# Delta rule and two MLP layers on one core: order of the start and of the first block rewritten

## The chip, the cores and the metric

One core of a Trainium2 chip. The metric is the device time of one execution in microseconds (us).

## The reference, cut to what matters

```python
k_n = k / (norm(k) + 1e-6)                       # q, k, v: 4 batches, 8 heads, 768 steps, 48 wide
for t in range(S):
    y[t] = q[t] @ state                          # state: 48x48 per batch and head
    state += beta[t] * outer(k_n[t], v[t] - k_n[t] @ state)
x = y as [3072 tokens, 384]
x = elu(x @ w_in) @ w_out                        # 384 -> 2048 -> 384
out = swish_1.702(x @ w_in2) @ w_out2
```

## The kernel before

**The work.** The 768 steps are cut into 12 chunks of 64 (`NC`), two chunks to a pass (`NP` = 6 passes of 128 steps). A pass begins with two Gram products (`gram`, L169, k against k, 128 small matmuls on PE each, evacuated by ACT at L182), from which `inverse` (L187) makes the norms and inverts 32x32 triangular blocks on DVE: `take` L205 (transpose), `diag` L210, `root` L221 to L223 and three times `better` L227 to L230 (a square root by Newton's steps), `norm` L234 to L242, `scale` L246, 14 row steps L262/L267 (passes 0 to 2, "fine"), `finish` L271/L272, `turn` L278. For the fine passes `join16` puts 16-wide halves together (transpose L292, `left` L299, `right` L307 to L309). Then a chunk's steps (`chunk`, from L315): `kq` (L342, with a masking on DVE at L348), `t2` L355, `m1` L364, `m2` L379, `nv` L332, `ks` L395/L400, `w` L408/L413, `state` L423/L426, `y` L434/L439, `out` (transposes L454, split into a high and a low part at L459/L460). Chunk c needs the state of chunk c-1.

**The layers.** The MLP runs in 192 units: for either layer, for 6 blocks of 512 tokens, for 16 slices of the hidden width. A unit is `up` (9 matmuls 128x512, L531, into a bank of PSUM), the activation (ACT L540, L541, DVE L544, ACT L553, DVE L556) and, two units later (`LAG`), `down` (9 matmuls, L565). Weights arrive as 64-bit words (`raw`, 768 KB a slice) and are made into a high and a low part by `prep`: `rebase` (ACT L489), `shift` and `rest` (DVE L496, L499), `high` (ACT L506), `low` (DVE L510). Unit t of the first block can't start before slice t is converted; later blocks of the layer use the same weights.

**The order.** It is written by hand in `schedule`, and each engine's queue is served in that order. Before unit 0 stands a start: loads, Gram products, `inverse` of pass 0, both chunks of pass 0 (chunk 1 without its `state`) and 20 of the 48 conversion steps. From unit 0 on four lists give what is put in at each unit: `fill` (after the activation's first half, mainly DVE work), `mid` (before `down`), `end` (after it); `spread` shares out a list over units by given sizes. In the block of units 0 to 15 the code puts the other 28 conversion steps (units 0 to 7), `inverse` of pass 1 (units 0 to 6), the chunks 2 and 3 (units 1 to 14, most of it from unit 8), the Gram products of pass 2 (units 8 and 10) and 3 (13 and 15), and `inverse` of pass 2 from unit 11. Block 1 (units 16 to 31) has chunks 4 and 5, still with `join16`, and `inverse` of pass 3 from unit 19. From unit 32 a block has two chunks, two Gram products and no joins.

**Buffers.** The chunk steps share one double bank of PSUM (`wide`, tile ps_w) and one single bank (`bank`, ps_b; in the start also the units' two h banks). The units' three accumulators acc0 to acc2 stand unused until unit 2. SP issues all loads, in order; the first ones are k of chunks 0 and 1, then q, weights, v at once.

Of the kernel before, what the change touches and what calls it, by code (L numbers as in the profile page):

```python
# [20 lines left out]
P = 128  # L21
# [10 lines left out]
class Kernel:  # L32
# [112 lines left out]
    def load_q(self, c):  # L145
# [41 lines left out]
    def inverse(self, p, spare=None):  # L187
# [29 lines left out]
        def root():  # L217

            a, q = small("na"), small("nb")
            s["a"], s["q"] = a, q  # L220
            v.tensor_scalar(out=a, in0=s["d"], scalar1=1e-30, scalar2=None, op0=ALU.max)  # L221
            v.tensor_scalar(out=q.bitcast(U32), in0=a.bitcast(U32), scalar1=1, scalar2=None, op0=ALU.logical_shift_right)
            v.tensor_scalar(out=q, in0=q, scalar1=2.0**64 / 1.457, scalar2=None, op0=ALU.mult)  # L223

        def better():
            a, q = s["a"], s["q"]
            v.reciprocal(out=a, in_=q)  # L227
            v.tensor_tensor(out=a, in0=a, in1=s["d"], op=ALU.mult)
            v.tensor_tensor(out=a, in0=a, in1=q, op=ALU.add)
            v.tensor_scalar(out=q, in0=a, scalar1=0.5, scalar2=None, op0=ALU.mult)  # L230
# [50 lines left out]
        return [start, take, diag, root, better, better, better, norm, scale] + rows + [finish, turn]  # L281
# [33 lines left out]
    def chunk(self, c):  # L315
# [20 lines left out]
        def kq(ps=None):  # L336
            ps = self.wide() if ps is None else ps
            for u in range(8):
                for hf, ab in self.turns():
                    k = self.w_half(hf, ab)  # L340
                    r = 64 * (1 - k)
                    pe.matmul(  # L342
                        ps[self.tok(k), hf, 64 * u:64 * u + 64], g["kt"][r:r + D, 8 * hf + u, :],
                        g["x"][k][r:r + D, 8 * hf + u, :], start=True, stop=True,
                    )
            for k in range(2):
                r = self.tok(k)
                v.tensor_tensor(  # L348
                    out=g["x"][k][r], in0=ps[r].rearrange("p f (u t) -> p (f u) t", u=8),
                    in1=self.mask_p[r].unsqueeze(1).to_broadcast([64, 16, 64]), op=ALU.mult,  # L350
                )
# [50 lines left out]
        def w():  # L402
            ps = self.wide()
            z = s["z"][:, us, :]
            for u in range(8):
                for hf, ab in self.order():
                    k, t = self.w_half(hf, ab), self.tok(ab)
                    pe.matmul(  # L408
                        ps[self.tok(k), hf, hs(u)], z[t, 8 * hf + u, :], st["r"][t, hf, hs(u)],
                        start=True, stop=True,  # L410
                    )
            for k in range(2):
                act.copy(su[k][self.tok(k)], ps[self.tok(k), :, 0:HB])  # L413
# [14 lines left out]
        def y():  # L428
            st["y"] = ap.tile([P, 2, HB], F32, name="y", tag="ry", bufs=2)
            ps = self.wide()  # L430
            for u in range(8):
                for hf, ab in self.order():
                    k = self.w_half(hf, ab)
                    pe.matmul(  # L434
                        ps[self.tok(ab), hf, hs(u)], g["x"][k][:, 8 * hf + u, :], su[k][:, hf, hs(u)],
# [3 lines left out]
            act.copy(  # L439
                st["y"].rearrange("p i (f x) -> p f i x", f=2),  # L440
                ps[:, :, 0:HB].rearrange("p f (i x) -> p f i x", i=2),
            )
# [19 lines left out]
        return dict(nv=nv, t2=t2, m1=m1, kq=kq, m2=m2, ks=ks, w=w, state=state, y=y, out=out)  # L462
# [179 lines left out]
    def schedule(self):  # L642

# [3 lines left out]
        mid, end, fill = {}, {}, {}  # L647
# [19 lines left out]
        names = ("nv", "t2", "m1", "kq", "m2", "ks", "w", "state", "y", "out")  # L667
# [34 lines left out]
        loads[1]()  # L702
        self.load_v(0)
        self.load_v(1, "ry", 2)
        self.load_kn(0)
        loads[2]()
        self.constants()
        self.gram(0, self.grp[0]["kt"])
        self.gram(1, self.grp[1]["kt"])
        for f in steps[0:3]:  # L710
            f()
        ch[0]["kq"]()
        for f in steps[3:8]:
            f()
# [15 lines left out]
        convert(2)  # L730
# [47 lines left out]
        for slot, c, name in (  # L778
# [3 lines left out]
        ):  # L782
# [7 lines left out]
        for p in range(2, NP):  # L790
            o = base[p - 1]
            a, b = 2 * p, 2 * p + 1
            for slot, c, name in (
# [5 lines left out]
                at(end if slot % 2 else mid, u, ch[c][name])  # L799
# [32 lines left out]
        for t in range(len(units) + self.LAG):  # L832
# [44 lines left out]
    def sizes(self, p):  # L877

        rows = [0.14 + j * (15 - j) / 240 for j in range(1, 15)] if p in self.FINE else [0.14 + j * (31 - j) / 480 for j in range(1, 31)]
        return [0.1, 1.9, 0.2, 0.7, 1.0, 1.0, 1.0, 1.7, 1.2] + rows + [1.4, 1.9]  # L880
# [102 lines left out]
```

## Time and profile before

| | us |
|---|---|
| median of 3 runs (lowest, highest) | 1098.32 (1095.07, 1101.81) |
| the profiled execution | 1102.94 |
| its span | 1101.2 |
| busy: PE, DVE, ACT, POOL | 1015.4, 594.8, 452.4, 49.2 |
| granted TensorE clock, mean | 0.966 |

Of the profiled execution 1.7 us lie outside the span. The busy shares are averages over a start without large matmuls, a first block in which three kinds of work meet, and a long part in which PE is busy nearly without a break.

### The profile page before, as it was taken

The numbers are of one execution on the slowest core, as the hardware profiler recorded it, in microseconds if no ns is written. First come the engines' busy times: TensorE is split into PE (matmuls) and PEld (weight loads), VectorE is DVE, ScalarE is ACT, GpSimd is POOL, SyncE is SP. The second block draws the span as 40 slices with busy tenths as digits, with TensorE's granted clock in tenths as the row PEclk, the third lists the DMA queues.
The fourth block names the chain that finished last, engine by engine and source line by source line (L and its number), as shares of the span: only waits on it lengthen the run. The fifth ranks groups of instructions, "written<-read, shape, count | busy, mean of one in ns | idle before, by whom it ended". The sixth has DMA issues, their size and how long they took to land.

```text
span 1101.2 us, 26885 instructions
## 1 busy us (share of the span) xinstructions
PE 1015.4 (92%) x12136; PEld 866.1 (79%) x12136; DVE 594.8 (54%) x1047; ACT 452.4 (41%) x733; POOL 49.2 (4%) x65
## 2 busy tenths in 40 slices
PE   4377688897999999999999899999999999999997
PEld 4365567776888788888888788899999999999996
DVE  3648971665577677777643366673333333333332
ACT  2245343343445534444544466553333333233332
POOL 2000000000000100000000000010000001000000
PEclk9997876998999999999999999999999999999999
DMA  8435001140113022121110190101002020020101
GB/s 271 178 153 162 1 2 36 36 126 32 60 52 94 18 82 60 51 77 49 42 31 1 73 407 37 58 1 35 24 1 58 1 58 1 1 58 1 29 1 29
DMA packets 20563, 68.41 MB, mean 62 GB/s; under 512 B 3552, under 2 KB 6624, under 8 KB 20448
## 3 DMA queue, kind: packets, MB, share of 16 engines
q1 hardware_dynamic: 20448, 66.69, 18.2%
q8 instruction: 95, 1.56, 0.6%
q14 instruction: 20, 0.16, 0.0%
HBM read 57.25 MB, written 9.44 MB: 61 GB/s over the span
## 4 chain that ended last, share of the span: by engine, by line
PE 86%; DVE 8%; issue 3%; ACT 2%; DMA 1%; ACTq 0%; DVEq 0%
PE h L531 35%; PE acc L565 17%; PE acc L576 9%; PE accn L576 9%; PE ps_w L434 3%; PE ps_w L342 2%; PE ps_w L180 2%; PE ps_w L423 1%; PE ps_b L364 1%; PE ps_b L379 1%; PE ps_w L395 1%; PE ps_w L408 1%; DVE tmp L262 1%; DVE W L267 1%; DVE x L348 1%
## 5 line engine op out<-in xcount | busy, mean ns | idle before, releaser
L531 PE MATMUL h<-xh,wt 128*128 128x512 f32 x1152 | 401.6, 403 | 0.6 <-ACT xh L459 0.6
L531 PEld LDWEIGHTS h<-xh,wt 128*128 128x128 f32 x1152 | 220.0, 191 | 47.0 <-ACT xh L459 1.0
L531 PE MATMUL h<-xl,wt 128*128 128x512 f32 x576 | 229.4, 398 | 0.0
L565 PE MATMUL acc<-gh,wt 128*128 128x512 f32 x576 | 203.7, 408 | 3.1 <-ACT xo L629 2.6
L553 ACT CAST gh<-t 128x512 fp32r<-128x512 f32 x192 | 119.2, 621 | 174.0 <-DVE t L544 117.9
L556 DVE TENSOR_TENSOR gl<-t,gh 128x512 fp32r<-128x512 f32 x192 | 138.4, 721 | 67.9 <-PE acc L576 29.5
L550 DVE TENSOR_TENSOR t<-t,h 128x512 f32<-128x512 f32 x96 | 66.0, 688 | 180.3 <-ACT t L547 180.1
L547 ACT ACTIVATE t<-h 128x512 f32<-128x512 f32 x96 | 57.4, 598 | 198.9 <-PE h L531 198.9
L565 PEld LDWEIGHTS acc<-gh,wt 128*128 128x128 f32 x576 | 112.6, 196 | 28.3 <-ACT xo L629 3.0
L565 PE MATMUL acc<-gl,wt 128*128 128x512 f32 x288 | 117.3, 407 | 15.1 <-DVE gl L556 15.1
L531 PEld LDWEIGHTS h<-xl,wt 128*128 128x128 f32 x576 | 110.0, 191 | 19.6 <-DVE xl L460 0.3
L540 ACT ACTIVATE t<-h 128x512 f32<-128x512 f32 x96 | 57.3, 597 | 136.4 <-PE h L531 136.0
L544 DVE SCALAR_TENSOR_TENSOR t<-t,h 128x512 f32<-128x512 f32 x96 | 65.4, 681 | 72.4 <-ACT t L541 72.0
L576 PE MATMUL acc<-wt,gh 128*128 128x384 f32 x384 | 98.4, 337 | 0.0
L576 PE MATMUL accn<-wt,gh 128*128 128x384 f32 x384 | 98.0, 336 | 0.0
L565 PEld LDWEIGHTS acc<-gl,wt 128*128 128x128 f32 x288 | 56.5, 196 | 28.5 <-DVE gl L556 17.6
L576 PEld LDWEIGHTS accn<-wt,gh 128*128 128x128 f32 x384 | 70.9, 188 | 5.5
L576 PEld LDWEIGHTS acc<-wt,gh 128*128 128x128 f32 x384 | 70.3, 188 | 2.8
L576 PE MATMUL acc<-wt,gl 128*128 128x384 f32 x192 | 64.8, 338 | 0.0
L576 PE MATMUL accn<-wt,gl 128*128 128x384 f32 x192 | 64.7, 337 | 0.0
L541 ACT ACTIVATE t<-t 128x512 f32<-128x512 f32 x96 | 60.7, 632 | 3.1
L593 POOL TENSOR_TENSOR xl<-x1r,xh 128x512 fp32r<-128x512 f32 x18 | 24.1, 1338 | 415.8 <-ACT xh L592 322.1
(126 smaller groups left out, 983.2 us busy)
## 6 DMA issues: line engine op xcount, KB each, us to landing
raw<-in_w SPq DMA_DIRECT2D x32, 768.0 KB, 9.9
kt<-in_kT SPq DMA_DIRECT2D x12, 512.0 KB, 4.7
x<-in_qT SPq DMA_DIRECT2D x24, 256.0 KB, 5.0
kg<-in_kT SPq DMA_DIRECT2D x10, 512.0 KB, 4.1
vn<-in_vn SPq DMA_DIRECT2D x12, 384.0 KB, 3.4
kn<-in_kn SPq DMA_DIRECT2D x12, 384.0 KB, 3.2
x1d<-xo SPq DMA_DIRECT2D x12, 384.0 KB, 2.8
x1r<-x1d SPq DMA_DIRECT2D x6, 768.0 KB, 4.6
```

The lines of the kernel that those rows point to most:

```text
L434: pe.matmul(ps[self.tok(ab), hf, hs(u)], g["x"][k][:, 8 * hf + u, :], su[k][:, hf, hs(u)], start=True, stop=True,)
L531: nc.tensor.matmul(hps, wt[:, part, k * P:(k + 1) * P], src[:, k, c], start=(i == 0), stop=(i == 3 * NK - 1))
L540: nc.scalar.activation(out=t, in_=hps, func=AF.Relu, scale=-1.0)
L541: nc.scalar.activation(out=t, in_=t, func=AF.Exp, scale=-1.0)
L544: nc.vector.scalar_tensor_tensor(out=t, in0=t, scalar=-1.0, in1=hps, op0=ALU.add, op1=ALU.max)
L547: nc.scalar.activation(out=t, in_=hps, func=AF.Sigmoid, scale=1.702)
L550: nc.vector.tensor_tensor(out=t, in0=t, in1=hps, op=ALU.mult)
L553: nc.scalar.copy(gh, t)
L556: nc.vector.tensor_tensor(out=gl, in0=t, in1=gh.bitcast(F32), op=ALU.subtract)
L565: self.nc.tensor.matmul(acc[c], wt[:, part, DM + c * P:DM + (c + 1) * P], src, start=(m == 0 and i == 0), stop=(m == NM - 1 and i == 2),)
L576: self.nc.tensor.matmul(acc[w], src[:, c], wt[:, part, DM:2 * DM], start=(m == 0 and i == 0), stop=(m == NM - 1 and i == 2),)
L593: nc.gpsimd.tensor_tensor(out=xl[:, c, :], in0=st["raw"][:, c, :], in1=xh[:, c, :].bitcast(F32), op=ALU.subtract)
```

## The change

- **Loads.** `constants` is called first. After k of chunks 0 and 1 and beta, no load is issued until both Gram products of pass 0 are evacuated: `load_q(0, gate=True)` has ACT write one column of the tile that the next load fills, and SP's later loads queue behind that one.
- **Banks.** In the start the first two Gram products, `kq` and `y` of chunk 0 and `w` of chunks 0 and 1 use pairs of the accumulators (`banks`) in place of `wide`; Gram and `w` are evacuated half by ACT, half by DVE. `kq` is split: its masking is a step of its own, `mask`.
- **Square root.** For passes 0 and 1 `root` is one ACT Sqrt with a DVE maximum, followed by one `better`; passes 2 to 5 keep three. `better` has 3 instructions where it had 4. ACT's table at the start is that of Sqrt; Exp follows before unit 0.
- **Order of the start.** `inverse` of pass 0 runs through without the masks between its steps; the start has 5 conversion steps instead of 20, and of pass 1's `inverse` the steps up to and with `scale` (`meanwhile`). The rest of that `inverse` (14 row steps, `finish`, `turn`) goes to units 0 to 2.
- **First block.** Three conversion steps (one slice) in each of units 0 to 13, `rebase` behind `end` in a list of its own (`tail`); joins of chunks 2 and 3 in units 2 to 5 (before 7 and 8), their steps from unit 2 to 14; Gram products of pass 2 in units 3 and 6, its `inverse` from unit 9; `inverse` of pass 3 from unit 21 (before 19).

```diff
@@ constants
-        nc.scalar.activation(out=self.one, in_=self.one, func=AF.Exp)
+        nc.scalar.activation(out=self.one, in_=self.one, func=AF.Sqrt)
@@ load_q
+        if gate:
+            self.nc.scalar.copy(g["x"][0][:, 0, 0:1], self.one)
+    def banks(self, i):
+        return [self.ps_m.tile([P, TB], F32, name=f"acc{j}", tag=f"acc{j}", bufs=1) for j in (i, i + 1)]
@@ gram
-        self.nc.scalar.copy(z, ps)
+        if c < 2:
+            self.nc.scalar.copy(z[:, 0], ps[0])
+            self.nc.vector.tensor_copy(z[:, 1], ps[1])
+        else:
+            self.nc.scalar.copy(z, both)
@@ inverse: root, better
+            if p < 2:
+                nc.scalar.activation(out=q, in_=s["d"], func=AF.Sqrt)
+                v.tensor_scalar(out=q, in0=q, scalar1=1e-20, scalar2=None, op0=ALU.max)
+                return
...
-            v.tensor_tensor(out=a, in0=a, in1=s["d"], op=ALU.mult)
-            v.tensor_tensor(out=a, in0=a, in1=q, op=ALU.add)
-            v.tensor_scalar(out=q, in0=a, scalar1=0.5, scalar2=None, op0=ALU.mult)
+            v.scalar_tensor_tensor(out=a, in0=a, scalar=0.5, in1=s["d"], op0=ALU.mult, op1=ALU.mult)
+            v.scalar_tensor_tensor(out=q, in0=q, scalar=0.5, in1=a, op0=ALU.mult, op1=ALU.add)
@@ w (in the start)
+                    act.copy(su[k][self.tok(k), 0], ps[0][self.tok(k), 0:HB])
+                    v.tensor_copy(su[k][self.tok(k), 1], ps[1][self.tok(k), 0:HB])
@@ schedule
-        def convert(n):
-            for f in conv[0:n]:
+        first = [self.later(lambda p=p: self.inverse(p, lambda: turned(p)), len(self.sizes(p))) for p in range(2)]
+
+        beside = list(zip(self.sizes(1), first[1]))
+        beside = beside[0:6] + [(0.8, f) for f in conv[0:5]] + beside[6:]
+
+        def meanwhile(us):
+            while beside and us > 0.0:
+                size, f = beside.pop(0)
                 f()
-            del conv[0:n]
-
+                us -= size
+
+        self.constants()
         self.load_kt(0)
         self.load_kt(1)
         self.a_start(0)
-        self.load_q(0)
-        loads[0]()
+        self.gram(0, self.grp[0]["kt"], self.banks(0))
+        self.gram(1, self.grp[1]["kt"], self.banks(1))
+
+        self.load_q(0, gate=True)
         self.load_kg(2)
         self.load_q(1)
-        loads[1]()
-        self.load_v(0)
-        self.load_v(1, "ry", 2)
-        self.load_kn(0)
-        loads[2]()
-        self.constants()
-        self.gram(0, self.grp[0]["kt"])
-        self.gram(1, self.grp[1]["kt"])
-        for f in steps[0:3]:
-            f()
-        ch[0]["kq"]()
-        for f in steps[3:8]:
+        for f in first[0]:
             f()
         self.a_start(1)
         self.gram(2, self.kg)
         self.load_kg(3)
-        for f in loads[3:10]:
+        self.load_v(0)
+        for f in loads[0:2]:
             f()
-        for f in bases[0:7]:
+        self.load_kn(0)
+        self.load_v(1, "ry", 2)
+        for f in loads[2:4]:
             f()
+        bases[0]()
+        self.gram(3, self.kg)
+        bases[1]()
+        ch[0]["kq"]()
         ch[1]["kq"]()
-        for f in steps[8:]:
-            f()
-        self.gram(3, self.kg)
         join[0][0]()
         join[0][1]()
         join[1][0]()
         join[1][1]()
-        convert(2)
+        for f in loads[4:8]:
+            f()
+        meanwhile(2.1)
+        ch[0]["mask"]()
+        meanwhile(0.7)
         join[0][2]()
         ch[0]["t2"]()
         ch[0]["m1"]()
-        convert(1)
+        ch[1]["mask"]()
         join[1][2]()
-        ch[1]["t2"]()
-        ch[1]["m1"]()
         ch[0]["nv"]()
         ch[0]["m2"]()
         ch[0]["ks"]()
+        ch[1]["t2"]()
         ch[0]["w"]()
+        ch[1]["m1"]()
+        ch[0]["state"]()
+        ch[0]["y"]()
         ch[1]["m2"]()
-        convert(2)
+        bases[2]()
+        bases[3]()
+        nc.scalar.activation(out=self.one, in_=self.one, func=AF.Exp)
         ch[1]["nv"]()
-        ch[0]["state"]()
-        convert(1)
-        ch[0]["y"]()
         self.load_kn(1)
-        for f in loads[10:16]:
+        for f in loads[8:16]:
             f()
-        convert(2)
         ch[1]["ks"]()
         ch[0]["out"]()
-        for f in bases[7:9]:
-            f()
-        convert(2)
         ch[1]["w"]()
-        convert(4)
-        for f in bases[9:12]:
-            f()
+        meanwhile(2.4)
         ch[1]["y"]()
-        convert(4)
+        meanwhile(4.0)
         ch[1]["out"]()
...
-        spread(fill, 0, 8, conv)
-        spread(end, 0, 3, bases[12:])
+        spread(fill, 0, 3, [f for _, f in beside], [size for size, _ in beside])
+        for m in range(2, NM):
+            at(fill, m - 2, *conv[3 * m - 1:3 * m + 2])
+            at(tail, m - 2, *bases[m + 2:m + 3])
+            taken[m - 2] = 0.6
+        at(fill, NM - 2, conv[-1])
         at(mid, 0, ch[1]["state"], lambda: self.load_kn(2))
-        spread(fill, 0, 7, self.later(lambda: self.inverse(1, lambda: turned(1)), len(self.sizes(1))), self.sizes(1))
-        for slot, c, i in ((14, 2, 0), (14, 2, 1), (15, 3, 0), (15, 3, 1), (16, 2, 2), (17, 3, 2)):
+        for slot, c, i in ((5, 2, 0), (5, 2, 1), (7, 2, 2), (8, 3, 0), (8, 3, 1), (10, 3, 2)):
             at(end if slot % 2 else mid, slot // 2, join[c][i])
         for slot, c, name in (
-            (3, 2, "kq"), (5, 3, "kq"), (13, 2, "nv"), (16, 2, "t2"), (16, 2, "m1"), (17, 3, "t2"), (17, 3, "m1"),
-            (18, 2, "m2"), (18, 2, "ks"), (19, 3, "m2"), (20, 2, "w"), (22, 2, "state"), (22, 3, "nv"), (23, 2, "y"),
-            (25, 3, "ks"), (26, 3, "w"), (27, 3, "state"), (28, 3, "y"), (28, 2, "out"), (29, 3, "out"),
+            (4, 2, "kq"), (4, 2, "mask"), (7, 2, "nv"), (9, 2, "t2"), (9, 2, "m1"), (10, 3, "kq"), (10, 3, "mask"),
+            (11, 2, "m2"), (12, 3, "t2"), (12, 3, "m1"), (13, 2, "ks"), (14, 3, "m2"), (15, 2, "w"), (17, 2, "state"), (17, 3, "nv"),
+            (18, 2, "y"), (20, 3, "ks"), (22, 3, "w"), (24, 3, "state"), (25, 2, "out"), (26, 3, "y"), (28, 3, "out"),
         ):
-            at(end if slot % 2 else mid, slot // 2, ch[c][name])
-        at(end, 9, lambda: self.load_v(3))
-        at(end, 11, lambda: self.load_kn(3))
+            u = slot // 2
+            at(end if slot % 2 else mid, u, ch[c][name])
+            taken[u] = taken.get(u, 0.0) + self.VECTOR.get(name, 0.0)
...
-                self.passes(at, spread, end, fill, p, (8, 10), (11, o + 2), lambda: turned(2))
+                self.passes(at, spread, end, fill, p, (3, 6), (9, o + 2), lambda: turned(2))
             else:
                 grams = (13, 15) if p == 3 else (o - 16, o - 14)
-                self.passes(at, spread, end, fill, p, grams, (o - 13, o + 3))
+                self.passes(at, spread, end, fill, p, grams, (o - 11 if p == 3 else o - 13, o + 3))
```

## Rows read from the trace of the kernel before

**Rows 1.** Busy time by stretch: PE, PEld, DVE, ACT, POOL; clock, DMA share, GB/s.
```profile
0.00:42.70 42.70, 15.83 (x640) 14.32 (x640) 22.88 (x60) 11.37 (x13) 5.66 (x16) 1.00 0.81 288
42.70:92.40 49.70, 32.82 (x1164) 30.60 (x1165) 23.19 (x33) 22.47 (x35) 2.08 (x4) 0.88 0.42 149
92.40:154.50 62.10, 46.38 (x574) 35.59 (x574) 59.81 (x109) 24.79 (x38) 1.59 (x2) 0.85 0.08 22
154.50:236.30 81.80, 72.34 (x1702) 58.02 (x1692) 33.72 (x72) 30.87 (x50) 3.66 (x6) 0.83 0.22 67
236.30:343.20 106.90, 99.86 (x1715) 81.02 (x1709) 70.15 (x146) 44.21 (x75) 3.34 (x5) 0.95 0.17 49
343.20:436.80 93.60, 93.47 (x1454) 76.08 (x1453) 67.71 (x140) 44.10 (x72) 3.34 (x5) 1.00 0.20 61
...
```

**Rows 2.** PE's waits before unit 0: total us, times, longest.
```profile
PE h L299 <- DVE xl L278: 10.2, 1, 10.2
...
PE ps_w L434 <- DVE su L426: 2.1, 1, 2.1
```

**Rows 3.** PE's waits in units 0 to 7.
```profile
PE acc L565 <- DVE gl L556: 13.6, 5, 5.4
```

**Rows 4.** Timeline of the start: start, us, engine, line; in brackets the idle before.
```profile
0.81 1.28 ACT L72 ACT_TABLE_LOAD   x1 [0.81 <-PEq L971]
...
7.79 1.60 PE L180 MATMUL ps_w<-kt 48*32 48x64 f32 x95 [1.10 <-ACT z L182]
...
12.79 0.74 PE L180 MATMUL ps_w<-kt 48*32 48x64 f32 x33 [3.40 <-issue]
...
14.63 1.94 DVE L205 STREAM_TRANSPOSE W<-z 128x1024 f32<-128x1024 f32 x1 [14.63 <-ACT z L182]
...
20.95 0.18 DVE L221 TENSOR_SCALAR na<-dg 128x32 f32<-128x32 f32 x1
...
24.17 3.68 PE L342 MATMUL ps_w<-x,kt 48*64 48x64 f32 x64 [1.10 <-ACT z L182]
...
24.77 0.18 DVE L234 TENSOR_SCALAR nb<-nb 128x32 f32<-128x32 f32 x1
...
27.90 2.46 DVE L348 TENSOR_TENSOR x<-ps_w,mask_p 64x1024 f32<-64x1024 f32 x2 [1.64 <-PE ps_w L342]
...
30.39 1.23 DVE L246 TENSOR_TENSOR W<-W,na 128x1024 f32<-128x1024 f32 x1
...
40.75 1.91 DVE L278 STREAM_TRANSPOSE xl<-W 128x1024 f32<-128x1024 f32 x1
...
47.74 0.66 PE L299 MATMUL ps_b<-xl,z 32*32 32x16 f32 x34 [1.85 <-issue]
```

**Rows 5.** The page's DMA issues: KB each, median us from issue to landing.
```profile
raw<-in_w SPq DMA_DIRECT2D x32, 768.0 KB, 9.9
...
kg<-in_kT SPq DMA_DIRECT2D x10, 512.0 KB, 4.1
```

**Rows 6.** Groups of DVE's instructions in units 0 to 15: busy us, mean ns.
```profile
L510 DVE TENSOR_TENSOR wt<-w,wt 128x768 fp32r<-128x768 f32 x11 | 10.5, 952 | 0.0
L556 DVE TENSOR_TENSOR gl<-t,gh 128x512 fp32r<-128x512 f32 x15 | 10.2, 683 | 0.8 <-ACT gh L553 0.7
...
L499 DVE SCALAR_TENSOR_TENSOR w<-raw,w 128x768 uint32<-128x768 uint32 x10 | 9.6, 957 | 0.3
...
L496 DVE TENSOR_SCALAR w<-raw 128x768 uint32<-128x768 uint32 x9 | 5.1, 562 | 0.3
```

**Rows 7.** PE's timeline at the starts of units 9, 10 and 11.
```profile
173.84 0.80 PE L531 MATMUL h<-xh,wt 128*128 128x512 f32 x1
...
187.18 0.50 PE L531 MATMUL h<-xh,wt 128*128 128x512 f32 x1
...
194.22 0.50 PE L531 MATMUL h<-xh,wt 128*128 128x512 f32 x1
```

**Rows 8.** PE's timeline in unit 20.
```profile
273.26 1.92 PE L379 MATMUL ps_b<-m,t 32*32 32x32 f32 x64 [3.06 <-DVE z L309]
```

More of the change, by code (lines that the diff above doesn't have):

```diff
@@ L143, in load_kg, with load_q @@
         self.nc.sync.dma_start(self.kg, self.kT[c])
-    def load_q(self, c):
+    def load_q(self, c, gate=False):
         g = self.grp[c]
         g["x"] = [self.ap.tile([P, 16, 64], F32, name=f"x{k}", tag=f"x{k}", bufs=2) for k in range(2)]
+        if gate:
+            self.nc.scalar.copy(g["x"][0][:, 0, 0:1], self.one)
         for k in range(2):
@@ L166, in a_start @@
         s["z"] = self.ap.tile([P, 32, 64], F32, name="z", tag="z", bufs=2)
+    def banks(self, i):
+        return [self.ps_m.tile([P, TB], F32, name=f"acc{j}", tag=f"acc{j}", bufs=1) for j in (i, i + 1)]
     def gram(self, c, kt, ps=None):
         s = self.pas[c // 2]
-        ps = self.wide() if ps is None else ps
+        if ps is None:
+            both = self.wide()
+            ps = [both[:, hf] for hf in range(2)]
         for u in range(8):
@@ L280, in inverse @@
         rows = [lambda j=j: step16(j) for j in range(1, 15)] if fine else [lambda j=j: step(j) for j in range(1, 31)]
-        return [start, take, diag, root, better, better, better, norm, scale] + rows + [finish, turn]
+        return [start, take, diag, root] + [better] * (1 if p < 2 else 3) + [norm, scale] + rows + [finish, turn]
     def join16(self, c, home):
@@ L334, in nv, with kq @@
             )
-        def kq(ps=None):
-            ps = self.wide() if ps is None else ps
+        def kq():
+            if first:
+                ps = self.banks(0)
+            else:
+                both = self.wide()
+                ps = [both[:, hf] for hf in range(2)]
             for u in range(8):
@@ L342, in kq, with mask @@
                     pe.matmul(
-                        ps[self.tok(k), hf, 64 * u:64 * u + 64], g["kt"][r:r + D, 8 * hf + u, :],
+                        ps[hf][self.tok(k), 64 * u:64 * u + 64], g["kt"][r:r + D, 8 * hf + u, :],
                         g["x"][k][r:r + D, 8 * hf + u, :], start=True, stop=True,
                     )
+            st["kq"] = ps if first else both
+        def mask():
+            ps = st.pop("kq")
             for k in range(2):
                 r = self.tok(k)
[L348 to L351, printed above, removed]
+                for f, part in (((0, ps[0]), (1, ps[1])) if first else ((None, ps),)):
+                    if f is None:
+                        o, i = g["x"][k][r], part[r].rearrange("p f (u t) -> p (f u) t", u=8)
+                    else:
+                        o, i = g["x"][k][r, 8 * f:8 * f + 8], part[r].rearrange("p (u t) -> p u t", u=8)
+                    v.tensor_tensor(
+                        out=o, in0=i, in1=self.mask_p[r].unsqueeze(1).to_broadcast(list(i.shape)), op=ALU.mult,
+                    )
         def t2():
@@ L402, in w @@
         def w():
-            ps = self.wide()
+            if self.early:
+                ps = self.banks(0)
+            else:
+                both = self.wide()
+                ps = [both[:, hf] for hf in range(2)]
             z = s["z"][:, us, :]
@@ L412, in w @@
             for k in range(2):
-                act.copy(su[k][self.tok(k)], ps[self.tok(k), :, 0:HB])
+                if self.early:
+                    act.copy(su[k][self.tok(k), 0], ps[0][self.tok(k), 0:HB])
+                    v.tensor_copy(su[k][self.tok(k), 1], ps[1][self.tok(k), 0:HB])
+                else:
+                    act.copy(su[k][self.tok(k)], both[self.tok(k), :, 0:HB])
         def state():
@@ L429, in y @@
             st["y"] = ap.tile([P, 2, HB], F32, name="y", tag="ry", bufs=2)
-            ps = self.wide()
+            if first:
+                ps = self.banks(0)
+            else:
+                both = self.wide()
+                ps = [both[:, hf] for hf in range(2)]
             for u in range(8):
@@ L434, in y @@
                     pe.matmul(
-                        ps[self.tok(ab), hf, hs(u)], g["x"][k][:, 8 * hf + u, :], su[k][:, hf, hs(u)],
+                        ps[hf][self.tok(ab), hs(u)], g["x"][k][:, 8 * hf + u, :], su[k][:, hf, hs(u)],
                         start=True, stop=True,
                     )
[L439 to L442, printed above, removed]
+            to = st["y"].rearrange("p i (f x) -> p f i x", f=2)
+            if first:
+                for hf in range(2):
+                    act.copy(to[:, hf], ps[hf][:, 0:HB].rearrange("p (i x) -> p i x", i=2))
+            else:
+                act.copy(to, both[:, :, 0:HB].rearrange("p f (i x) -> p f i x", i=2))
         def out():
@@ L460, in out @@
                 v.tensor_tensor(out=xl[:, :, dst], in0=src, in1=xh[:, :, dst].bitcast(F32), op=ALU.subtract)
-        return dict(nv=nv, t2=t2, m1=m1, kq=kq, m2=m2, ks=ks, w=w, state=state, y=y, out=out)
+        return dict(nv=nv, t2=t2, m1=m1, kq=kq, mask=mask, m2=m2, ks=ks, w=w, state=state, y=y, out=out)
     def x_tiles(self, key):
@@ L642, in schedule @@
     def schedule(self):
+        nc = self.nc
         units = [(kind, p, 0, TB, m) for kind in "tn" for p in range(NP) for m in range(NM)]
         base = [NM * p for p in range(2 * NP)]
-        mid, end, fill = {}, {}, {}
+        mid, end, fill, tail = {}, {}, {}, {}
         def at(where, u, *fns):
@@ L665, in spread @@
                 room -= size * part
-        names = ("nv", "t2", "m1", "kq", "m2", "ks", "w", "state", "y", "out")
+        names = ("nv", "t2", "m1", "kq", "mask", "m2", "ks", "w", "state", "y", "out")
         ch = {c: dict(zip(names, self.later(lambda c=c: list(self.chunk(c).values()), len(names)))) for c in range(NC)}
@@ L798, in schedule @@
                 u = o + slot // 2
-                at(end if slot % 2 else mid, u, ch[c][name])
+                at(end if slot % 2 else mid, u, ch[c][name], *([ch[c]["mask"]] if name == "kq" else []))
                 taken[u] = taken.get(u, 0.0) + self.VECTOR.get(name, 0.0)
@@ L851, in schedule @@
                 rest[2]()
-                for f in end.pop(t, []):
+                for f in end.pop(t, []) + tail.pop(t, []):
                     f()
@@ L879, in sizes @@
         rows = [0.14 + j * (15 - j) / 240 for j in range(1, 15)] if p in self.FINE else [0.14 + j * (31 - j) / 480 for j in range(1, 31)]
[L880 removed]
+        return [0.1, 1.9, 0.2, 0.7] + [0.8] * (1 if p < 2 else 3) + [1.7, 1.2] + rows + [1.4, 1.9]
     VECTOR = {"kq": 0.15, "t2": 0.26, "m1": -0.44, "m2": -0.44, "ks": -0.1, "w": -0.44, "state": 0.15, "y": -0.74, "out": 0.17}
```

6 lines of the change are left out of this document (4 added, 2 removed).

## The prediction

> **What bounds the kernel now.** I read the busy time by stretch first [rows 1], with stretches cut at units 0, 8, 16 and 32, and look for those in which PE is not full at a full clock. From unit 32 on there is nothing to gain that this change touches: 93.5 us busy of 93.6 for a block, clock 1.00. Before that three stretches are loose. The start (92.4 us) has PE busy for half of its time, on small products. In units 0 to 7 (62.1 us) DVE is busy for 59.8: DVE is the bound, and the waits say so too, with 13.6 us in which `down` waits for `gl` [rows 3]. Units 8 to 15 (81.8 us) have DVE at 33.7 and PE at 72.3, but at a clock of 0.83: what DVE kept out of the first half was crowded into the second. Units 16 to 31 take 106.9 us against 93.6 for the next 16.
>
> Then the waits of the start [rows 2] and its timeline [rows 4]: the longest wait is that of the first join for the transposed inverse, 10.2 us. So the chain there is loads, Gram products, `inverse` of pass 0 on DVE from 14.63 to 42.66, then the chunks' steps from PE to ACT or DVE and back until unit 0 at 92.4.
>
> **The first Gram products.** The second one begins at 7.79, stops at 9.39 with nothing in the profile that it waits for ("issue"), and goes on at 12.79 [rows 4]. It is a stop after some 220 small products; a like one at 47.74, when the loads are over, is 1.85 us. I read both as PE's supply of code, longer while loads stream. With the loads held back I take 1.9 instead of 3.4: -1.5. Two pairs of banks and half copies save some 0.5 at the 1.10 us in front of the second product and 0.5 at its evacuation. Sum -2.5 (0 to -4): `take` begins at about 12. [...]
>
> **The first inverse.** It lasts 28.0 us now [rows 4]. The two masks between its steps go: 2.46 each, with 1.64 of waiting in front (one of the two is shown), 8.2 in all. `root` and three `better`, 20.95 to 24.77, become one ACT Sqrt, a maximum and one `better`: 3.8 down to about 1.4. Left are 17.4, so `turn` ends at 12 + 17.4 = 29.4, against 42.66.
>
> **What is late next.** PE can't use all of it. Its queue has Gram 2, Gram 3 and both `kq` in front of the first join now. The load for Gram 2 is issued after the gate (about 12.2) and two q loads, at 13.5; with 4.1 to landing [rows 5] Gram 2 runs from 17.6 to 19.7 (95 such products took 1.60 [rows 4], so 128 take 2.1); the load of Gram 3 reuses its buffer: 19.9 + 4.1 + 2.1 = 26.1. `kq` takes 3.68 [rows 4]: 29.8. The second `kq` needs the double bank, so ACT's copy of Gram 3, and that stands behind the first `rebase`, which waits for a weight load issued at about 20 with up to 9.9 to landing [rows 5]. So the second `kq` starts between 29.8 and 32 and the join between 33.5 and 35.7: I take 34.5. Of 13 us won on DVE, 8 arrive: the join starts at 34.5 instead of 42.7.
>
> **From the join to unit 0** lie 49.7 us now. Less: `m1` of chunk 1 and its code no longer stand ahead of `m2` of chunk 0, -3; `y` of chunk 0 has banks of its own and skips the 2.1 us wait for `state` [rows 2]; halves of `w` on two engines, two times about -0.75. More: in front of chunk 1's `out` DVE now does one `better`, `norm`, five conversion steps and `scale`, some 7.4 us, beside `y`'s 3.65 products, copy and transposes (6 us): +1.4. ACT's Exp table (1.28 [rows 4]) and two `rebase` stand ahead of `out` of chunk 0 and so ahead of the copies that chunk 1's `y` needs: +2. Code: the small products now run while twelve weight loads stream, at 12 to 40 and again from 60; each stop may grow by 1.5, as above, if PE isn't waiting anyway: 0 to +6, I take +1. Sum 47.5 (42 to 54). Unit 0 begins at 82 instead of 92.4: -10.4 (-18 to 0). [...]
>
> **Units 0 to 2** stay DVE's. A slice of weights is 0.56 + 0.96 + 0.95 = 2.5, and a unit's own two (the `gl` row stands for both) 1.4 [rows 6]. Three of each are 11.7. The rest of pass 1's inverse, from the end of `scale` at 31.62 to 42.66 [rows 4], is 11.0; one mask 2.5 and two `state` adds 1.9 come to it: 27. Unit 3's own slice is ready a little earlier: 26 us for three units.
>
> **Units 3 to 15** should be PE's. DVE then has some 4 us a unit of slices and activation and has lost pass 1's inverse. PE's work in the block is unchanged: 46.4 + 72.3 busy at clocks of 0.85 and 0.83 [rows 1] is about 99.5 us at full clock. The first three units hold 13 of it, so 86.5 remain. Some is lost to waits and to a low clock after them: block 1 with the same mixture lost 106.9 - 99.9 x 0.95 = 12, of which I give 4 to a stop treated below. I take 8.5. The block: 26 + 86.5 + 8.5 = 121 against 143.9 (92.4 to 236.3): -23. Bounds: nothing lost and DVE beside PE from unit 1 on, 106 (-38); twice block 1's loss, 137 (-7). DVE's whole work there, 93.5 us in the two stretches [rows 1] with 14 of pass 1 gone, 12 of conversion and some 5 of pass 2 come, is below either.
>
> **Block 1.** In unit 20 `m2` waits 3.06 us for a join's subtraction [rows 8], which stands in DVE's queue behind a mask and the first steps of pass 3's inverse; the clock falls after it. That inverse now begins a unit later than this place, and `better` is shorter. -4 (0 to -8). From unit 32 on nothing changes but three short DVE instructions a pass beside a full PE: 0.
>
> **The sum:** -10.4 - 23 - 4 = -37 on the profiled execution's 1102.9 (span 1101.2 and 1.7 around it): 1065.5. That execution stands 4.6 above the median of the runs, 1098.3, from which the same sum gives 1061. The clock's falls, which make most of such differences, lie in the stretches that are rewritten; I take 1062.
>
> **Rivals.** (1) Code. If the stops in the start all grow (+6, the far end), and if the small products, now spread over units 2 to 8 with one to three groups in each, stop there as at 47.74 (1.85, one in every second unit, four in all, each followed by a low clock costing as much again: +15), the time is about 1083. For it: every stop named "issue" stands in small products; against: wide products leave time to fetch. (2) All loose time goes: start -15, block 0 -33, block 1 -6, -54 in place of -37: 1045. For it: units 32 to 47 do the like at 93.5 of 93.6; against: block 1 doesn't. [...] (4) The change doesn't do what it says: the gate holds no load back long enough to matter, the banks free nothing, and DVE stays the bound to unit 7. Then the start gives 0, block 0 -4, block 1 -4: 1091. For it: DVE's whole work in block 0 hardly falls; against: in units 8 to 15 it is idle for half of the time.
>
> **Chances.** Forecast with its own range 1052 to 1073: 0.56; (1) 0.2; (2) 0.16; (3) 0.04; (4) 0.04. A measurement of this kernel tells about 1%, 11 us, from no change; only (4) lies within it and only (3) above. Faster 0.92, same 0.04, slower 0.04. The range for 8 in 10 goes down past (2), as far as the good ends of its terms (-18, -38, -8, one of them half: about 1036), and up to (1): 1036 to 1083.
>
> **What would show it.** Right: `take` at 11 to 13, `turn` done at 28 to 31, first join 33 to 36 with `kq` just in front, unit 0 at 78 to 86; units 0 to 2 in 24 to 28 us with DVE full; units 3 to 15 near 95 with a clock above 0.9; unit 32 about 37 us earlier than at 343.2, and the rest unchanged. Wrong: a start over 90, waits for `gl` after unit 4, many "issue" waits of PE in units 2 to 8, or a clock below 0.8 there.

## The result and the profile after

The changed kernel takes 1070.76 us (median of 4 runs, 1067.46 to 1071.66) where the kernel before took 1099.5 beside it (4 runs): 0.974 of the time, 95% interval 0.970 to 0.978, some 29 us less. The profiled execution took 1067.46 us (span 1065.8). The two profiled executions lie 35.5 apart, because that of before stood above its median and this one is the fastest of its runs; stages are compared on these two, medians for the whole.

The same stretches as in [rows 1], the first unit now at 83.1, unit 3 at 108.2, unit 8 at 151.0, unit 16 at 204.3, unit 32 at 307.6. Busy time by stretch, columns as in [rows 1]:

```profile
0.00:32.70 32.70, 15.66 (x640) 14.30 (x640) 21.36 (x51) 6.70 (x10) 5.65 (x17) 1.00 0.67 227
32.70:83.10 50.40, 29.96 (x1169) 27.69 (x1165) 22.41 (x39) 17.14 (x32) 3.65 (x6) 0.96 0.52 208
83.10:108.20 25.10, 18.46 (x292) 13.76 (x292) 23.98 (x50) 8.82 (x13) 0.00 (x0) 0.75 0.50 125
108.20:151.00 42.80, 39.85 (x1191) 32.01 (x1180) 28.34 (x40) 26.22 (x42) 2.07 (x4) 0.96 0.08 25
151.00:204.30 53.30, 50.06 (x800) 40.10 (x797) 42.44 (x85) 29.88 (x45) 1.58 (x2) 0.97 0.23 76
204.30:307.60 103.30, 99.84 (x1714) 81.28 (x1709) 66.71 (x132) 44.32 (x75) 3.34 (x5) 0.95 0.18 54
307.60:401.50 93.90, 93.39 (x1453) 75.93 (x1452) 68.68 (x142) 43.78 (x72) 3.34 (x5) 1.00 0.20 61
```

Unit 0 begins 9.3 us earlier (83.1 for 92.4). Block 0 takes 121.2 for 143.9, so 22.7 less. Block 1 takes 103.3 for 106.9, so 3.6 less on these two executions. Together 35.6, and from unit 32 on nothing changes. DVE's work in block 0 is about what it was: 23.98 + 28.34 + 42.44 = 94.8 us for 93.5. It lies elsewhere: DVE is the bound for 25 us (23.98 of 25.10), where before it was for 62.1 (59.8), and behind that PE is busy for 94% of its time at a clock of 0.96 to 0.97, where units 8 to 15 had 0.83.

PE's waits, total, times, longest; up to "..." those before unit 0 [rows 2], then units 0 to 2, then the largest of units 3 to 15 [rows 3]:

```profile
PE ps_w L188 <- DMA kg<-in_kT: 11.2, 2, 7.2
PE acc L188 <- DMA kt<-in_kT: 4.7, 1, 4.7
PE ps_b L315 <- issue: 4.3, 1, 4.3
PE h L573 <- DVE xl L502: 3.0, 1, 3.0
PE h L315 <- issue: 2.4, 1, 2.4
PE h L323 <- issue: 1.9, 1, 1.9
...
PE h L573 <- DVE wt L552: 5.9, 2, 5.4
...
PE ps_w L496 <- DVE su L462: 2.7, 1, 2.7
```

The 10.2 us for `xl` at the first join are gone. In their place PE waits for the two loads of Gram 2 and 3 while DVE still inverts; the join then begins 3.5 us behind the end of the inverse, when PE is through with its own queue (Gram 3 and both `kq`). After that PE stops with nothing named ("issue"), above all inside the joins (L315, L323). Waits of `down` for `gl` (13.6 us) are gone altogether. Timeline of the start, and of the place where the clock still falls in block 1:

```profile
7.59 2.42 PE L188 MATMUL acc<-kt 48*32 48x64 f32 x128 [0.80 <-DVE z L192]
...
10.89 1.90 DVE L217 STREAM_TRANSPOSE W<-z 128x1024 f32<-128x1024 f32 x1
...
13.08 1.26 POOL L223 TENSOR_SCALAR_AFFINE_SELECT W<-W 128x1024 f32<-128x1024 f32 x1 [8.16 <-DVE dg L222]
13.30 1.07 DVE L234 TENSOR_SCALAR nb<-nb 128x32 f32<-128x32 f32 x1 [0.29 <-ACT nb L233]
...
17.24 2.06 PE L188 MATMUL ps_w<-kg 48*32 48x64 f32 x128 [7.23 <-DMA kg<-in_kT]
...
23.25 2.04 PE L188 MATMUL ps_w<-kg 48*32 48x64 f32 x128 [3.95 <-DMA kg<-in_kT]
...
25.22 3.68 PE L362 MATMUL acc<-x,kt 48*64 48x64 f32 x64
...
27.20 1.99 DVE L294 STREAM_TRANSPOSE xl<-W 128x1024 f32<-128x1024 f32 x1
...
29.14 3.68 PE L362 MATMUL ps_w<-x,kt 48*64 48x64 f32 x64 [0.24 <-ACT z L194]
...
32.75 1.47 PE L315 MATMUL h<-xl,z 32*32 32x16 f32 x94
...
36.62 0.66 PE L315 MATMUL h<-xl,z 32*32 32x16 f32 x33 [2.40 <-issue]
...
42.81 0.66 PE L315 MATMUL ps_b<-xl,z 32*32 32x16 f32 x33 [4.29 <-issue]
...
44.09 0.18 DVE L234 TENSOR_SCALAR nb<-nb 128x32 f32<-128x32 f32 x1 [9.01 <-ACT nb L233]
...
55.41 1.17 PE L407 MATMUL h<-xl,xh 32*32 32x32 f32 x36 [1.59 <-issue]
...
220.05 0.84 PE L323 MATMUL ps_b<-w 16*32 16x16 f32 x78 [1.25 <-issue]
...
221.16 0.39 PE L573 MATMUL h<-xl,wt 128*128 128x512 f32 x1
...
222.85 0.63 PE L573 MATMUL h<-xl,wt 128*128 128x512 f32 x1
...
238.67 0.56 PE L407 MATMUL ps_b<-m,t 32*32 32x32 f32 x22 [0.53 <-DVE z L325]
```

The second Gram product (7.59) runs through in 2.42 us; before, it stopped for 3.40 [rows 4]. `take` starts at 10.89, `turn` ends at 29.2 (42.66 before), and the first join starts at 32.75, right behind `kq`. The wait in unit 20 [rows 8] went from 3.06 to 0.53.

### The profile page after: what moved, and what is told of

It reads as the page before. It is cut to its first block, busy times and chain, and to the rows that moved or that the text cites. A ratio compares the mean times of both kernels' runs of the same rounds, so it can differ in the third digit from the quotient of the medians.

```text
span 1065.8 us, 26850 instructions
## 1 busy us (share of the span) xinstructions
PE 1001.8 (94%) x12136; PEld 855.6 (80%) x12136; DVE 590.9 (55%) x1021; ACT 451.4 (42%) x739; POOL 49.1 (5%) x65
## 4 chain that ended last, share of the span: by engine, by line
PE 89%; DVE 5%; issue 2%; DMA 2%; ACT 1%; SPq 0%; ACTq 0%; DVEq 0%
PE h L573 37%; PE acc L607 18%; PE acc L618 10%; PE accn L618 9%; PE ps_w L362 2%; PE ps_w L474 2%; PE ps_w L459 1%; PE ps_b L392 1%; PE ps_w L188 1%; PE ps_b L407 1%; PE ps_w L423 1%; PE ps_w L440 1%; PE ps_b L315 1%; PE ps_b L323 1%; DVE w L541 1%
## 5 line engine op out<-in xcount | busy, mean ns | idle before, releaser
L607 PE MATMUL acc<-gh,wt 128*128 128x512 f32 x576 | 198.6, 399 | 3.1 <-ACT xo L671 2.6
L607 PEld LDWEIGHTS acc<-gh,wt 128*128 128x128 f32 x576 | 109.2, 190 | 27.7 <-ACT xo L671 3.0
L607 PE MATMUL acc<-gl,wt 128*128 128x512 f32 x288 | 113.3, 394 | 0.0
L607 PEld LDWEIGHTS acc<-gl,wt 128*128 128x128 f32 x288 | 54.7, 190 | 10.2
L635 POOL TENSOR_TENSOR xl<-x1r,xh 128x512 fp32r<-128x512 f32 x18 | 24.1, 1337 | 415.9 <-ACT xh L634 322.1
```

Source lines behind the costliest of these rows:

```text
L607: self.nc.tensor.matmul(acc[c], wt[:, part, DM + c * P:DM + (c + 1) * P], src, start=(m == 0 and i == 0), stop=(m == NM - 1 and i == 2),)
L635: nc.gpsimd.tensor_tensor(out=xl[:, c, :], in0=st["raw"][:, c, :], in1=xh[:, c, :].bitcast(F32), op=ALU.subtract)
```

## The experiments

Each ran beside the kernel before on the same chip; kernels of one group shared those runs: the first four (before: median 1100.1), the next four (1099.6), the last two (1097.6). The groups ran on three chips, so across groups the ratio counts beside the time.

**The changed kernel once more.** No edit, as the yardstick of the first group.

> The changed kernel once more, unaltered, as the measure for the runs beside it. 1066 to 1072 us; unit 0 at 83.1 us, unit 3 at 108.2, unit 16 at 204 and unit 32 at 308, each within 1 us up to unit 3 and within 4 us behind it, where the clock falls at places that differ between executions.

1068.45 us (6 runs, 1066.39 to 1078.05), ratio 0.973 (0.970 to 0.977). Unit 0 at 82.1, unit 16 at 203.5, unit 32 at 308.3: stage times repeat to about 1.5 us.

**Loads not held back.**

```diff
-        self.load_q(0, gate=True)
+        self.load_q(0)
```

> The gate alone is undone: the q loads and the load of Gram 2 go out behind those of k at once. My theory: the second Gram product stops for code up to 3 us longer (its end at 10.0 becomes 11 to 13), the inverse ends 1 to 3 us later (29.2 becomes 30 to 32), but Gram 2, Gram 3 and both kq move 5 us ahead, so the join begins at 30 to 32.5 instead of 32.75, and the loads that stream while the joins want code end earlier: unit 0 at 78 to 83 instead of 83.1, the whole the same or up to 4 us faster. Rival (the gate pays): what it saves on the first inverse arrives at unit 0, so without it unit 0 comes at 85 to 87 and the whole is 2 to 4 us slower.

1072.18 us (5 runs, 1070.88 to 1073.36), ratio 0.975 (0.973 to 0.978). From its timeline:

```profile
13.58 0.74 PE L188 MATMUL acc<-kt 48*32 48x64 f32 x33 [4.68 <-issue]
...
15.20 1.90 DVE L217 STREAM_TRANSPOSE W<-z 128x1024 f32<-128x1024 f32 x1
...
29.18 0.80 PE L188 MATMUL ps_w<-kg 48*32 48x64 f32 x34 [6.09 <-issue]
```

The stop in the second Gram product is back, 4.68 us, and `take` starts at 15.20 instead of 10.6 to 10.9. The inverse ends at 33.5, but the join starts only at 37.40 (32.76 in the run above): what holds it is PE's own queue, with a stop of 6.09 in the middle of Gram 3. Unit 0 comes only 2.1 later (84.2), because the stops behind the join are then shorter (2.35, 1.55 and 1.66, for 3.44, 3.47 and 1.66 in the run above). So the gate gains 4.6 at the join, and more than half of it is taken back before unit 0; at unit 16 the two profiles stand level (203.3 and 203.5). My expectation that the join would begin at 30 to 32.5 fell, and so did the rival's 85 to 87 for unit 0. Its 2 to 4 us for the whole are left open: the median is 3.7 above the repeat's and 1.4 above that of the changed kernel's first four runs.

**Four weight loads later.** Raw slices 4 to 7, issued behind the joins, are issued with 8 to 15 instead, behind a later key load.

```diff
-        for f in loads[4:8]:
-            f()
...
-        for f in loads[8:16]:
+        for f in loads[4:16]:
             f()
```

> The weight loads 4 to 7 (3 MB) go behind the wait for chunk 0's state, so that no load streams after about 34 us. Theory (code under load): PE's stops named issue in the joins of the start, 2.4, 4.3 and 1.9 us, come down to 1.9 each or less, the second one above all; unit 0 at 79 to 81 instead of 83.1. Rival (small products outrun the code supply with or without loads): the stops stay within half a microsecond each and unit 0 within 1 us of 83.1. A loss would come from the 12 loads behind 64 us ending some 8 us later, at the conversions of units 2 and 3.

1065.45 us (6 runs, 1059.99 to 1067.29), ratio 0.968 (0.965 to 0.971). PE's timeline from the join on:

```profile
33.53 1.47 PE L315 MATMUL h<-xl,z 32*32 32x16 f32 x94
35.15 0.65 PE L315 MATMUL h<-xl,z 32*32 32x16 f32 x33 [0.15 <-issue]
35.60 0.22 PE L315 MATMUL ps_b<-xl,z 32*32 32x16 f32 x3
35.65 0.21 PE L315 MATMUL h<-xl,z 32*32 32x16 f32 x1
35.66 1.40 PE L315 MATMUL ps_b<-xl,z 32*32 32x16 f32 x91
38.88 0.66 PE L315 MATMUL ps_b<-xl,z 32*32 32x16 f32 x33 [1.83 <-issue]
...
51.22 1.17 PE L407 MATMUL h<-xl,xh 32*32 32x32 f32 x36 [1.33 <-issue]
```

The products are the same as in the changed kernel; only loads have gone from beside them. The first two stops fall from 3.44 and 3.47 to 0.15 and 1.83, and unit 0 comes at 79.1, 3.0 earlier than in the repeat, as the theory had it (79 to 81); the median is 3.0 lower too. Between two stops lie 33 + 3 + 1 + 91 = 128 products, each with its weight load. That is 256 instructions. In this run the first stop is 0.15, and the four behind it, up to 51.22, take 1.3 to 1.8 us each; the longest was 4.3 in the changed kernel, with loads beside it (DMA share 1.03 from 36.62 to 40.21), and 6.1 without the gate.

That these stops are waits for code can be read from the trace itself. The page counts packets on a DMA queue of the kind "instruction":

```profile
q8 instruction: 95, 1.56, 0.6%
```

These are 95 packets of 16 KB for PE's 12136 products and as many weight loads, so about one for 256 instructions (24272 / 95 = 255.5). By the records of single packets in the changed kernel's trace, five of its stops behind the join (2.40, 4.29, 1.93, 1.44 and 1.59) end 1.3 to 1.6 us behind the end of such a packet: the first three packets run from 34.08 to 35.18, from 40.21 to 41.23 and from 44.43 to 45.30, and PE goes on at 36.62, 42.81 and 46.65. In the kernel before, the stops of 3.40 and 1.85 [rows 4] end 1.5 and 1.6 behind one (11.29 for 12.79, 46.18 for 47.74). A packet takes about 1 us beside the loads (1.10 and 1.02) as without them (0.87). What comes later beside the loads is its start: 3.6 us after PE goes on from the stop before (36.62 to 40.21, DMA share 1.03), and 1.6 once they are over (42.81 to 44.43, DMA share 0.03). Not every stop named "issue" is of this kind: one of 0.78 in the changed kernel (it ends at 57.36) stands 36 products after the last one, and the packet before it had ended 3.2 us earlier.

**Newton's root again.** Passes 0 and 1 with three `better` in place of Sqrt, ACT's table Exp from the start (two places of the edit are shown; the start also makes room on DVE for pass 1's two more steps).

```diff
-            if p < 2:
-                nc.scalar.activation(out=q, in_=s["d"], func=AF.Sqrt)
-                v.tensor_scalar(out=q, in0=q, scalar1=1e-20, scalar2=None, op0=ALU.max)
-                return
...
-        return [start, take, diag, root] + [better] * (1 if p < 2 else 3) + [norm, scale] + rows + [finish, turn]
+        return [start, take, diag, root] + [better] * 3 + [norm, scale] + rows + [finish, turn]
```

> The square root of passes 0 and 1 by ACT is undone: three Newton steps (in their shorter form) as in the other passes, ACT's table is that of Exp from the start, no second table load. My theory: DVE is 1.5 to 2.5 us later at the end of the first inverse (29.2 becomes 31 to 32), which PE's own queue covers, as both kq end at 32.8; then pass 1's two more steps cost DVE 1.6 us ahead of unit 0, and the Exp load of 1.5 us in front of chunk 0's out goes. Unit 0 at 82.5 to 85 (83.1 with Sqrt), the whole within 2 us of it. Rival (the Sqrt is worth its whole 2.4 us twice): unit 0 at 87 or later and the whole 4 us slower.

1071.21 us (6 runs, 1065.95 to 1072.51), ratio 0.974 (0.971 to 0.976). The inverse ends 2.3 later than in the repeat (31.2), but the join, 1.2 later (34.0), does not wait for it: it begins behind the second `kq`, and 0.9 of the 1.2 are there already where Gram 2 starts (17.94 for 17.00), for a reason that no run shows. Unit 0 comes 2.3 later (84.4), inside the theory's 82.5 to 85 and short of the rival's 87. The whole time, 2.8 above the repeat and 0.5 above the first four runs, can't be told from the changed kernel's.

**Pass 3's inverse from unit 19 again.**

```diff
-                self.passes(at, spread, end, fill, p, grams, (o - 11 if p == 3 else o - 13, o + 3))
+                self.passes(at, spread, end, fill, p, grams, (o - 13, o + 3))
```

> Undone alone: the inverse of pass 3 begins in unit 19 again instead of 21. Theory: in units 18 to 20 a join's subtraction stands in DVE's queue behind the mask and that inverse again, PE waits some 3 us for it and the clock falls behind the wait; units 16 to 31, 103 to 107 us in the runs of the changed kernel, take 106 to 110, the whole is 2 to 4 us slower. Rival (block 1's gain came from the shorter Newton steps or from where the clock fell): no wait over 1 us there and no difference in the whole beyond 1.5 us.

1070.44 us (5 runs, 1068.97 to 1075.85), ratio 0.975 (0.973 to 0.977). PE's longest wait in its block 1:

```profile
PE ps_b L407 <- DVE z L325: 2.9, 1, 2.9
```

The wait of [rows 8] is back at 2.9 us (0.5 with the change), so the rival's "no wait over 1 us" fell. What the wait costs is not shown. Block 1 takes 106.4 us for 103.3 and 104.8 in the two profiles of the changed kernel, but this profile is of the slowest of the five runs, and in the ten profiles of this study with the later inverse the block takes from 103.3 to 107.9. In the median it is 2 us above the repeat, and the intervals overlap.

**Conversion first in units 0 to 2.** On DVE the conversion of the next slice goes ahead of the rest of pass 1's inverse: the line `spread(fill, 0, 3, ...)` for that rest moves behind the three units' conversion steps.

> In units 0 to 2 the conversion of a slice goes ahead of the rest of pass 1's inverse on DVE, instead of behind it. Theory (DVE bounds the three units by its sum): the 5.4 us wait of unit 2 for its weights shrinks to under 2, but DVE's sum is the same, so unit 3 begins only 0 to 3 us earlier than 25.1 us behind unit 0, and what PE gains early it waits for later at the join that needs the inverse: the whole 0 to 3 us faster. Rival (the order on DVE makes the bound): unit 3 begins 5 us or more earlier and the whole is 4 us or more faster.

1070.2 us (4 runs, 1067.0 to 1072.36), ratio 0.973 (0.971 to 0.976). PE's waits in its units 0 to 2:

```profile
PE ps_b L315 <- DVE xl L294: 3.3, 1, 3.3
...
PE h L573 <- DVE wt L552: 1.6, 1, 1.6
```

The 5.4 us wait for `wt` shrinks to 1.6, and a wait of the next join for `turn` takes its place. Unit 3 begins 24.1 us after unit 0 with DVE busy for 22.4 of them (24.0 of 25.1 without the edit): DVE's work fills these units in whichever order it comes. The whole can't be told from the changed kernel's.

**The chunk steps in their old places.** Joins and steps of chunks 2 and 3 and the Gram products and inverse of pass 2 go to the units they had before; all else stays changed (first and last lines of the edit).

```diff
-        for slot, c, i in ((5, 2, 0), (5, 2, 1), (7, 2, 2), (8, 3, 0), (8, 3, 1), (10, 3, 2)):
+        for slot, c, i in ((14, 2, 0), (14, 2, 1), (15, 3, 0), (15, 3, 1), (16, 2, 2), (17, 3, 2)):
...
-                self.passes(at, spread, end, fill, p, (3, 6), (9, o + 2), lambda: turned(2))
+                self.passes(at, spread, end, fill, p, (8, 10), (11, o + 2), lambda: turned(2))
```

> The start and the conversions as changed, but the steps of chunks 2 and 3, their joins and the Gram products and inverse of pass 2 in the units where they stood before (most from unit 8). It shows what spreading them is worth by itself. Theory: PE's work in the block is the same, so units 3 to 7 take 4.1 to 5 us each (42 to 43 us in all now, then 21 to 26), units 8 to 15 grow from 53 to 70 to 80 us with stops for code among the crowded small products and a clock that falls after them; unit 16 at 207 to 213 instead of 203.5, the whole 3 to 10 us slower. Rival 1 (DVE's relief is all that counts): no slower than the changed kernel. Rival 2: as crowded as before, units 8 to 15 at 82 us and the whole 12 us or more slower.

1073.52 us (6 runs, 1072.4 to 1080.16), ratio 0.979 (0.976 to 0.981). Busy time of its units 0 to 2, 3 to 7 and 8 to 15:

```profile
84.70:109.80 25.10, 20.28 (x229) 15.54 (x229) 23.95 (x50) 8.94 (x13) 0.00 (x0) 0.76 0.51 130
109.80:133.80 24.00, 23.51 (x350) 18.98 (x346) 23.60 (x33) 17.82 (x27) 0.00 (x0) 1.00 0.01 1
133.80:210.20 76.40, 65.92 (x1703) 53.13 (x1693) 45.75 (x86) 38.77 (x60) 3.66 (x6) 0.93 0.24 72
```

The times of the three stretches and of unit 16 (210.2) are those that the theory gave. Block 0 takes 125.5 us, 4.3 more than with the steps spread out; units 3 to 15 take 100.4, where nine of the ten profiles with the steps spread out have 93.8 to 96.5 and one has 99.7. The median is 5.1 above the repeat's (2.8 above the first four runs), and a gain of 2% over the kernel before is no longer clear (0.976 to 0.981). So of the 22.7 us that block 0 gained, spreading the chunk steps brings some 4 to 5. The other 18 (143.9 - 125.5) come with what this run keeps: units 0 to 7 take 49.1 us here for 62.1 before (13 less; DVE 47.6 for 59.8), units 8 to 15 take 76.4 for 81.8 (5 less). The 13 belong to the conversion and inverse steps moved on DVE; which of the two weighs more was not separated.

**Both late loads and conversion first.** The edits of those two runs together.

> The weight loads 4 to 7 behind chunk 0's state together with the conversion ahead of pass 1's inverse in units 0 to 2. If the two gains are independent: unit 0 at 79 and the whole 3 us below the changed kernel plus what the order of DVE alone gives (0 to 3), so 1062 to 1066 where the changed kernel stands at 1068.5. If the late loads hold up the conversions of units 1 to 3 once these are asked for earlier, the gain of the order is lost and it stands at 1065 to 1068.

1064.03 us (4 runs, 1062.74 to 1066.55), ratio 0.968 (0.966 to 0.970), inside the 1062 to 1066 for independent gains: the late loads' gain, and at most 1 or 2 us on top. Unit 0 came at 80.8, not at 79: the first stop in the joins was 1.52 here, 0.15 with the late loads alone.

**Gram 3's keys in a buffer of their own.** On top of the late loads, that load no longer waits for Gram 2 to have read its buffer.

```diff
-        self.gram(2, self.kg)
-        self.load_kg(3)
+        self.gram(2, kg2)
...
+        self.load_kg(3, spare[0][:, 0:1024].rearrange("p (u t) -> p u t", u=16))
```

> On the kernel with the late weight loads: the keys of Gram 3 get a buffer of their own (the lower part of a tile that only the joins use), so their load and those behind it no longer wait until Gram 2 has read the shared one. Theory (what is late behind the short inverse is PE's own queue, held up by that load): Gram 3 begins at 20 to 21 instead of 23.9, the second kq ends at 29.5 to 31 instead of 33.5, the join begins there, 1 us behind the end of the inverse, and unit 0 comes at 75 to 77 instead of 79.1; the whole 1061 to 1064 where the late loads alone gave 1065.5. Rival (the code supply takes it back, since PE no longer idles before the joins and the loads stream until 32): the stops at the joins grow by 2 us or more and unit 0 stays at 78 to 80, the whole within 1 us of 1065.5.

1065.73 us (6 runs, 1057.78 to 1068.44), ratio 0.968 (0.965 to 0.971). PE's timeline in front of the join:

```profile
21.24 1.59 PE L188 MATMUL ps_w<-xh 48*32 48x64 f32 x94 [1.59 <-DMA xh<-in_kT]
24.99 0.80 PE L188 MATMUL ps_w<-xh 48*32 48x64 f32 x34 [2.16 <-issue]
25.72 3.68 PE L362 MATMUL acc<-x,kt 48*64 48x64 f32 x64
...
33.51 2.00 PE L315 MATMUL h<-xl,z 32*32 32x16 f32 x127
```

Gram 3 starts at 21.24 instead of 23.87, and stops for 2.16 in its middle. The join starts at 33.51, where the late loads alone had it at 33.53. The load was only what the trace showed. Behind it stands, as I read it, PE's supply of code: the stop of 2.16 is named "issue" and stands in front of the last 34 products of Gram 3, as the 6.09 without the gate does. Unit 0 comes at 78.3 and the whole within 0.3 us of the late loads alone, as the rival had it, though the time was lost in Gram 3 and not at the joins.

**All three.** The late loads, the buffer and conversion first.

> The same with the conversion ahead of pass 1's inverse in units 0 to 2. The order of DVE alone gave nothing in the whole, so within 1.5 us of the run beside it; were unit 3 to follow unit 0 by 23 us or less (24 to 25 with that order so far), it would be DVE's order that pays once PE comes earlier.

1063.23 us (5 runs, 1060.49 to 1064.97), ratio 0.968 (0.965 to 0.970); unit 0 at 78.4, unit 16 at 197.2. The fastest median of the study, 5 us below the repeat of the changed kernel; but the kernel before was the fastest of the three in this group too, and the ratio is that of the late loads alone. Apart from those, no part of it can be told from none. It lies 2.5 below the run beside it, where I had expected 1.5 at most, with ranges that overlap; the sign that I had named for DVE's order, unit 3 within 23 us of unit 0, did not show (25.0).

## Why the prediction was right

The forecast was 1062 us, the median 1070.76, inside both ranges, in the upper part of the narrow one; on the profiled execution the sum was -37 and came out as -35.5. Part of that closeness is luck: by the medians the change is -28.7 (-31.6 in the group of the repeat), and the difference comes from which executions were profiled. The prediction lays such differences mostly to the clock's falls; the runs do not bear that out (two of the repeat took 1067.49 us at a mean clock of 0.968 and 1078.05 at 0.975). By its steps:

- **The first Gram products.** `take` at about 12 forecast, 10.89 found. The stop was put down to code supply while loads stream, and the run without the gate shows that: 4.68 us with loads, 0.43 or less in the runs that hold them back, and in the kernel before a packet of code ends 1.5 us ahead of the place where PE goes on (11.29 for 12.79). I had left 1.9 standing.
- **The first inverse.** 17.4 us forecast, 18.3 found (10.89 to 29.2). The difference is one small instruction, below: it takes 0.9 us more than the prediction's rows had for one of its size.
- **What is late next.** The times were right (Gram 2 17.2 for 17.6, end of Gram 3 25.3 for 26.1, join 32.75 for 34.5), and that PE's queue takes over from DVE too. The holder was not the load of Gram 3, as the step had it, or not that alone: with the load out of the way the join does not move, because PE then stops for 2.16 in Gram 3, which I read as code. The wait forecast for the second `kq` did not come: it starts at 29.14, 0.24 behind the first.
- **From the join to unit 0.** 47.5 forecast, 50.4 found (49.3 in the repeat). The term that was mis-sized is "Code: 0 to +6, I take +1". `m2` of chunk 0 ended 23.8 us behind the join (56.6); with four loads moved away it ended 18.9 behind (52.4), and unit 0 came 45.6 behind the join. So the loads beside the joins cost some 4 us there, in place of 1, and the other terms together were near (46.5 forecast without code, 45.6 found); one by one they were not separated. The count of twelve loads in that term is wrong too: eight were issued from 21.4 to 29.5 and eight from 65.0 on. The join, 1.75 earlier than forecast, and this way, 2.9 longer, partly cancel in unit 0 (83.1 for 82).
- **Units 0 to 2.** 26 forecast, 25.1 found, with DVE the bound as said.
- **Units 3 to 15.** 95 forecast, 96.1 found at a clock of 0.96 to 0.97, so the lost time came in the size taken from block 1.
- **Block 1.** -4 forecast, -3.6 found on the pair of profiles. The later inverse removes the wait named (2.9 us). That the block is faster by it is not shown: 106.9 before lies within the 103.3 to 107.9 of the ten profiles that have the later inverse.

Of the rivals, the first (code) holds in the start only: units 3 to 15 have stops named "issue" of 1.1 and 0.7 us and no more. The granted clock there was 0.96 to 0.97.

Open is what is left in block 1, 103.3 us for 93.9 in the next. In unit 19 PE runs at the lower level (granted clock 0.50) for 10.2 us from 222.2 on, some 2 us behind a stop of 1.25 in a group of small products, which ends 1.4 us behind a packet of code (218.67); a wide product then takes 0.63 us (222.85) where one just before took 0.39 (221.16). The kernel before has such stretches too (0.50 from 271.7 to 278.5), and in the eight other runs whose timeline was read there single wide products take 0.6 us and more (0.63 at 221.51 in the repeat); none was made to remove it.

## What to carry to other kernels

Here PE's bound in a stream of small products was, as the trace reads, the supply of its code: stops named "issue" with some 128 products between them, each ending 1.3 to 1.6 us behind the end of a packet on the queue of kind "instruction"; four loads moved away brought unit 0 from 82.1 to 79.1. So look for such stops, and keep bulk loads away from that stretch. When a wait is removed, work out the next two holders, not one: Gram 3 began 2.6 us earlier with its load out of the way, and the join stood at 33.51 for 33.53. Where an engine's work does not shrink, the time can still fall if the stretch in which that engine is the bound gets shorter: with DVE at 94.8 us of work for 93.5, block 0 went from 143.9 us to 121.2.

## What the hardware showed that was not expected

DVE's maximum in `root`, on 128x32 (L234), takes 1.07 us at 13.30 and 0.18 us at 44.09. The first begins inside POOL's select on 128x1024 (13.08, 1.26 long), the second has no POOL instruction beside it; the repeat has 1.08 and 0.18. With Newton's root another instruction of the same shape stands at that place and takes 1.12. So what is slow is the place, not the instruction. In the six profiles with the new start in which both were read (this one, the repeat, and the runs without the gate, with the late loads, with Newton's root and with all three) the instruction at that place ends 0.03 to 0.05 us behind the end of the select, as if it waited for it. Why, no run tells.
